# Unit 0's last product: planned fp32 columns, or rounded products in the mixed stretch

## The chip, the cores and the metric

One core of a Trainium2 chip runs the whole kernel. The metric is the time of one execution in device microseconds. The engines are TensorE (PE in the profile; PEld is its weight load), VectorE (DVE), ScalarE (ACT), GpSimd (POOL) and SyncE (SP), which issues most DMAs.

## What is computed

Three stages follow each other. Causal attention by blocks of 64 (4 batches, 8 heads, 576 positions, 64 wide) gives 2304 tokens of 512 values. A dense stage makes of each token

```python
h = np.maximum(np.maximum(x @ w1, x @ w2), x @ w3)   # 512 -> 768, three matrices
x2 = h @ w_out                                       # 768 -> 512
```

and a routed stage sends each row of x2 to two of eight experts (512 to 1024 to 512), chosen from the logits `x2 @ w_gate` and `x2 @ w_noise`. The weights of the dense stage arrive as 8-byte floats, and the kernel makes 4-byte ones of them itself.

## The kernel before

The 2304 tokens are nine units of 256. A dense unit has two parts. Its hidden part takes three pairs of 128 hidden columns (fp = 0, 1, 2); for each it makes the products with w1, w2 and w3 in one PSUM bank each and takes the maximum of the three. Its columns part multiplies the maxima with w_out for two tiles of 128 tokens (tt = 0, 1). The 2 x 8 gate columns are w_out times the gate matrices, and are appended to w_out, so that a unit gives its routing logits beside x2.

Nearly all products are "rounded": an operand is split into a high part (rounded to fp32r by ScalarE, `hh` for the maxima) and a low part (the difference, by GpSimd or VectorE, `hl`), and one product becomes three (high x high, high x low, low x high), accumulated in one bank. A unit's columns are then, for each tt and each half of the 528 columns, 6 x 3 products of 264 columns (`columns`, lines 791 to 793), followed by a ScalarE copy to an `x2` tile (line 796) and a store.

Unit 0 is made in another way. It is computed before the weights are split, with plain fp32 products, of which the trace shows two records each: `first_hidden` (line 589), `first_max` (ScalarE copy, then two VectorE maxima, into the three `hh` buffers), then for each tt `first_columns` with w_out and again with the 16 gate columns (line 606), a ScalarE copy and a store.

All this stands in the planned stretch, `start()`, at the beginning. There the order on each engine is written by a small planner (`Plan.run`). Each operation has an engine, a cost in microseconds, the operations it waits for, and a time by which its result is late (0.1, for loads 2.0). An operation's level is the longest sum of cost and lateness from it to the end; whenever an engine is free in the planner's own clock, it takes the ready operation with the highest level. Attention jobs 4 to 7 get a tail of 15 on their last operation, `EX`. The planned operations are:

- the loads of 24 weight pieces by SyncE (`LD`), and their conversion: `integers` on VectorE, `low_bits` on ScalarE, `join` on GpSimd (`AD`). Pieces 0 to 17 are w1 to w3, by fp; 18 to 23 are the six 128-row blocks of w_out;
- the early attention jobs 0 to 7 (`LQ` and `LV` load, then scores, exponentials, scaling, transposes, values, `EX`). Jobs 0 to 3 give unit 0's input, 4 to 7 unit 2's;
- unit 0, as above;
- the splits of the weights (`part`: ScalarE, line 580, then GpSimd, line 578), with w_out last, as it waits for the products of w2 and w3 and the splits of w2 and w3;
- the gate columns (`gate_turn`, `gate_copy`, `gate_product`, `gate_out`).

Until the first `first_hidden`, holes of TensorE are filled with warm-up products (line 137).

Behind the planned stretch comes the mixed one. Attention jobs 8 to 31 are written one after the other, and between their steps `filler` takes steps from a generator, `chain`, which goes through the other dense units (2, 4, 1, 6, 3, 5, 7). The toolchain's scheduler then lays out the instructions of each engine. It keeps the order of the planned operations among themselves, but may place others between them where their data and buffers are there. Attention outputs of units 2, 4, 6 and 8 go to a ring of six buffers (`xA`), of which unit 2 has four before the mixed stretch.

Of the kernel before, what the change touches and what calls it, by code (L numbers as in the profile page):

```python
# [7 lines left out]
F32 = mybir.dt.float32  # L8
F32R = mybir.dt.float32r
# [13 lines left out]
UT = 256  # L23
# [31 lines left out]
class Plan:  # L55
# [5 lines left out]
    def add(self, engine, cost, emit, deps=(), prio=0.0, take=None, give=None, late=0.1):  # L61
        self.ops.append((engine, cost, emit, tuple(deps), prio, take, give, late))
        return len(self.ops) - 1
# [49 lines left out]
def plain(ap):  # L113
    return ap.bitcast(F32)
# [3 lines left out]
def tile_attention_moe_moe(ctx, tc, qT, kT, v, w1, w2, w3, w_out, gates, noise, e1, e2, out):  # L118
# [113 lines left out]
    def bank(kind="m"):  # L232
        n, c = TAGS[kind]
        return (psS if n == "s" else psT).tile([128, 512], F32, name=n, bufs=c)
# [186 lines left out]
    def new_x(u, g):  # L421
        if u == 8:
            return keep.tile([128, 2, D], F32R, name="xs")
        if u == 0:
            if g % 2 == 0:
                XT["0"] = moe.tile([128, 2, UT], F32, name="hl", bufs=3)
            XT[u, g] = XT["0"][:, g % 2]
            return XT[u, g]

        if u == 5:  # L430
            XT[u, g] = att.tile([128, 2, UT], F32R, name=("qe", "kve", "pe", "pte")[g])
            return XT[u, g]
        r = 0 if u in RINGS[0] else 1
        n = 4 * RINGS[r].index(u) + g - XBUF[r]
        while n >= 0 and RINGS[r][n // 4] not in done:
            next(fill)
        XT[u, g] = moe.tile([128, 2, UT], F32R, name=("xA", "xB")[r], bufs=XBUF[r])
        return XT[u, g]
# [149 lines left out]
        for kt in range(4):  # L588
            nc.tensor.matmul(H0[-1][:, j], WP[MATS[m][0]][:, kt, f:f + 128], XT[0, kt], start=kt == 0, stop=kt == 3)

    M0 = []

    def first_max(fp, m):
        ps = H0[3 * fp + m]
        if m == 0:
            M0.append(moe.tile([128, 2, UT], F32, name="hh", bufs=3))
            nc.scalar.activation(M0[fp], ps, AF.Copy)
        else:
            nc.vector.tensor_max(M0[fp], ps, M0[fp])

    C0 = {}

    def first_columns(tt, w, n):
        ps = C0["p"] = bank()
        for ft in range(6):
            nc.tensor.matmul(ps[:, :n], M0[ft // 2][:, ft % 2, tt * 128:tt * 128 + 128], w[ft], start=ft == 0,
                             stop=ft == 5)

    def first_out(tt):
        x2 = C0[tt] = keep.tile([128, DM], F32, name="x2", bufs=2)  # L610
        nc.scalar.activation(x2, C0["p"], AF.Copy)

    def first_gates(tt):
        if "g" not in C0:
            C0["g"] = logits()
        nc.vector.tensor_copy(C0["g"][:, tt], C0["p"][:, :2 * E])

    def first_load(j, eng, half):
        i = at(j)
# [8 lines left out]
    def start():  # L628
# [71 lines left out]
            work(n, 10.0 + n)  # L700

        hid, mats = [], [[], [], []]
        prev = None
        for fp in range(3):
            for m in range(3):
                d = [AD[6 * fp + 2 * m], AD[6 * fp + 2 * m + 1]] + [EX[j] for j in range(4)]
                a = add("PE", 1.73, lambda fp=fp, m=m: first_hidden(fp, m, 0), d + hid[-1:], 100.0, take="t")
                b = add("PE", 1.73, lambda fp=fp, m=m: first_hidden(fp, m, 1), [a], 99.0)
                hid.append(b)
                mats[m].append(b)  # L710
                prev = add("DVE" if m else "ACT", 0.6, lambda fp=fp, m=m: first_max(fp, m), [b] + ([prev] if m else []),
                           24.0, give="t")
        sp = {}

        def part(key, n, i, j, src, deps, prio, cost):
# [26 lines left out]
            done_g = go[-1]  # L742
        so = [part(None, "o", f, slice(0, DM), WPO[f], mats[1] + mats[2] + sp[1] + sp[2], 55.0, 1.26) for f in range(6)]
        part(None, "o", slice(0, 6), slice(DM, NG), WPG, so + go, 55.0, 0.4)
        last = prev
        for tt in range(2):
            a = add("PE", 5.2, lambda tt=tt: first_columns(tt, WPO, DM), [last, prev] + [AD[n] for n in range(18, 24)], 100.0, take="t")
            last = add("ACT", 0.75, lambda tt=tt: first_out(tt), [a], 24.0, give="t")
            add("SP", 0.7, lambda tt=tt: store(0, tt, C0[tt]), [last], 24.0)
            a = add("PE", 1.3, lambda tt=tt: first_columns(tt, [WPG[:, ft] for ft in range(6)], 2 * E), [last] + go, 100.0, take="t")  # L750
            last = add("DVE", 0.2, lambda tt=tt: first_gates(tt), [a], 24.0, give="t")
        for j in range(4, 8):
            pl.tail[EX[j]] = 15.0
        return pl, idle, hid[0]
# [49 lines left out]
    def logits():  # L804
        return keep.tile([128, 2, 2 * E], F32, name="gl", bufs=2)

    def moe1(u):
        parts = []
        yield from hidden(u, parts)
        done.add(u)  # L810
        yield 0.01
        gl = logits()
        for tt in range(2):
            x2 = keep.tile([128, DM], F32, name="x2", bufs=2)
            for c in (0, 264):
                columns(parts, tt, c, 264, x2, gl)
                yield 2.0
            store(u, tt, x2)
        late.append(route(u, gl))
        yield 0.1  # L820


# [140 lines left out]
    ready = set()  # L963

    def chain():
        for u in CH:
            while u not in ready:
                yield None
            yield from moe1(u)
# [59 lines left out]
    psA.append(ph1.enter_context(tc.tile_pool(name="psA", bufs=1, space=bass.MemoryType.PSUM)))  # L1029
    init_route()  # L1030
    init_ids()
    late.append(route(0, C0["g"]))
    done.add(0)
    ready.add(2)
    load_scores(EJ[0])
    load_rest(EJ[0])
# [371 lines left out]
```

## Time and profile before

| | |
|---|---|
| median of three timed runs | 1019.64 us (1015.58 to 1020.12) |
| the profiled execution | 1013.09 us |
| its span, first to last instruction | 1011.3 us |
| TensorE: matmuls, weight loads busy | 982.2 us, 894.9 us |
| VectorE, ScalarE, GpSimd busy | 479.6 us, 424.6 us, 457.2 us |
| mean granted TensorE clock | 0.995 |

Matmuls are pipelined, so a record is longer than the step to the next one; the time that a run of matmuls takes is read from start times. The profile's times are counted from the start of the span.

### The profile page before, as it was taken

What the parts mean: (1) busy time and instruction counts of PE and PEld (TensorE: products, weight loads), DVE (VectorE), ACT (ScalarE), POOL (GpSimd) and SP (SyncE); (2) the same over time, 40 slices, a digit from 0 to 9 for tenths busy, and PEclk for the clock granted to TensorE, in tenths of its full rate; (3) what the DMA queues carried; (4) which work ended last, traced back from release to release, by engine and by line L of the source; (5) the groups of instructions that cost most, each with busy time, mean ns of one, the idle gap of its engine ahead of it and who ended that gap; (6) DMA issues with size and microseconds to landing.
All of it is one profiled execution on the core that took longest, in us unless ns stands there. A gap on an engine that the chain in (4) does not pass through costs nothing. (4 is left out here: it accounts for less than half of the span.)

```text
span 1011.3 us, 17379 instructions
## 1 busy us (share of the span) xinstructions
PE 982.2 (97%) x6557; PEld 894.9 (88%) x6557; DVE 479.6 (47%) x1320; ACT 424.6 (42%) x1005; POOL 457.2 (45%) x381
## 2 busy tenths in 40 slices
PE   8989999999999999999998899999999999999997
PEld 4776898999999999999997789899898989888895
DVE  6873658766688787863245331132222222222221
ACT  5687447555556666642122333332331314232210
POOL 2777132241324334331224487774755647574302
PEclk9999999999999999999999999999999999999999
DMA  8931315221012221212001466554434435342101
GB/s 257 297 124 52 109 36 198 69 56 43 25 56 69 64 60 35 70 37 97 23 22 53 130 218 192 176 173 151 159 105 152 144 120 190 98 171 85 53 19 57
DMA packets 76264, 107.32 MB, mean 106 GB/s; under 512 B 23672, under 2 KB 48248, under 8 KB 76176
## 3 DMA queue, kind: packets, MB, share of 16 engines
q1 hardware_dynamic: 63408, 75.97, 24.4%
q0 software_dynamic: 10592, 29.41, 8.9%
q8 instruction: 53, 0.87, 0.4%
q10 hardware_dynamic: 2176, 0.79, 0.3%
q14 instruction: 35, 0.29, 0.1%
HBM read 86.66 MB, written 20.53 MB: 106 GB/s over the span
## 5 line engine op out<-in xcount | busy, mean ns | idle before, releaser
L179 POOL TENSOR_TENSOR w<-rw,w 128x1536 fp32r<-128x1536 f32 (+1 forms) x45 | 141.1, 3145 | 73.6 <-ACT w L178 59.2
L178 ACT ACTIVATE w<-rw 128x1536 fp32r<-128x1536 f32 (+1 forms) x45 | 60.5, 1344 | 101.9 <-DMA rw<-in_e 53.2
L1138 PE MATMUL b<-xh,w 128*128 128x384 f32 (+7 forms) x272 | 87.5, 323 | 0.7 <-ACT xh L1128 0.7
L1139 PE MATMUL b<-xl,w 128*128 128x384 f32 (+7 forms) x272 | 87.5, 322 | 0.0
L1140 PE MATMUL b<-xh,w 128*128 128x384 f32 (+7 forms) x272 | 87.4, 322 | 0.0
L767 PE MATMUL t<-xA,w 128*128 128x256 f32 x288 | 82.5, 286 | 0.0
L768 PE MATMUL t<-xA,w 128*128 128x256 f32 x288 | 81.8, 284 | 0.0
L769 PE MATMUL t<-xA,w 128*128 128x256 f32 x288 | 81.5, 283 | 0.0
L1187 POOL DMA_INDIRECT out_rows<-y,isc x40 | 40.6, 1014 | 78.9 <-DVE y L1186 72.1
L1143 DVE SCALAR_TENSOR_TENSOR ht<-b,ht 128x384 fp32r<-128x384 f32 (+6 forms) x56 | 29.1, 519 | 96.6 <-ACT ht L1142 96.6
L782 POOL TENSOR_TENSOR hl<-hm,hh 128x512 fp32r<-128x512 f32 x21 | 27.5, 1311 | 98.4 <-ACT hh L781 98.2
L1140 PE MATMUL t<-xh,w 128*128 128x256 f32 x240 | 67.4, 281 | 0.0
L1139 PE MATMUL t<-xl,w 128*128 128x256 f32 x240 | 67.3, 281 | 0.0
L1182 PE MATMUL b<-w,ht 128*128 128x512 f32 (+1 forms) x168 | 67.0, 399 | 0.0
L1138 PE MATMUL t<-xh,w 128*128 128x256 f32 x240 | 66.9, 280 | 0.0
L1184 PE MATMUL b<-w,ht 128*128 128x512 f32 (+1 forms) x168 | 66.4, 395 | 0.0
L1183 PE MATMUL b<-w,ht 128*128 128x512 f32 (+1 forms) x168 | 66.3, 394 | 0.0
L271 POOL TENSOR_TENSOR Kl<-rk,Kh 128x576 fp32r<-128x576 f32 x16 | 23.2, 1451 | 93.6 <-ACT Kh L270 93.6
L1186 DVE SCALAR_TENSOR_TENSOR y<-b,idt,prev 128x512 f32<-128x512 f32 (+1 forms) x24 | 18.0, 750 | 97.8 <-PE b L1184 71.0
L767 PE MATMUL t<-xB,w 128*128 128x256 f32 x216 | 61.3, 284 | 0.0
L768 PE MATMUL t<-xB,w 128*128 128x256 f32 x216 | 61.3, 284 | 0.0
L769 PE MATMUL t<-xB,w 128*128 128x256 f32 x216 | 61.2, 283 | 0.0
(421 smaller groups left out, 3077.6 us busy)
## 6 DMA issues: line engine op xcount, KB each, us to landing
rw<-in_e SPq DMA_DIRECT2D x32, 768.0 KB, 4.7
w<-in_w SPq DMA_DIRECT2D x18, 512.0 KB, 9.2
rw<-in_e SPq DMA_DIRECT2D x16, 512.0 KB, 3.7
rv<-in_v SPq DMA_DIRECT2D x16, 320.0 KB, 2.9
rk<-in_kT SPq DMA_DIRECT2D x16, 288.0 KB, 3.4
x2d<-x SPq DMA_DIRECT2D x18, 256.0 KB, 2.2
out_rows<-x SPq DMA_DIRECT2D x9, 512.0 KB, 3.3
w<-in_w_out SPq DMA_DIRECT2D x6, 512.0 KB
```

What stands on the lines that cost most here:

```text
L178: nc.scalar.activation(t[:, 0, :c], r[:, :c], AF.Copy)
L179: nc.gpsimd.tensor_sub(t[:, 1, :c], r[:, :c], plain(t[:, 0, :c]))
L767: nc.tensor.matmul(ps[:, j], wh, x[:, 0], start=kt == 0, stop=False)
L768: nc.tensor.matmul(ps[:, j], wh, x[:, 1], start=False, stop=False)
L769: nc.tensor.matmul(ps[:, j], wl, x[:, 0], start=False, stop=kt == 3)
L1138: nc.tensor.matmul(p, wt1(e, 0, kt, f), th[:, kt, c0:c1], start=kt == 0, stop=False)
L1139: nc.tensor.matmul(p, wt1(e, 0, kt, f), tl[:, kt, c0:c1], start=False, stop=False)
L1140: nc.tensor.matmul(p, wt1(e, 1, kt, f), th[:, kt, c0:c1], start=False, stop=kt == 3)
L1182: nc.tensor.matmul(ps, a, wt2(e, 0, f), start=f == 0, stop=False)
L1183: nc.tensor.matmul(ps, a, wt2(e, 1, f), start=False, stop=False)
L1184: nc.tensor.matmul(ps, l, wt2(e, 0, f), start=False, stop=f == 7)
L1187: st = nc.gpsimd.indirect_dma_start(out=out, out_offset=bass.IndirectOffsetOnAxis(ap=isc[:n, e, c:c + 1], axis=0), in_=y, in_offset=None, ...
```

## The change

Unit 0's columns leave the plan. `first_columns`, `first_out` and `first_gates` go. The maxima go to two `hm` buffers instead of three `hh`, and two new operations split each pair: `first_high` (ScalarE) and `first_low` (VectorE). The low parts of the first two pairs use the two `xA` buffers that unit 2 leaves free, the third an `hl` buffer. Unit 0's columns are then made as those of the other units, by a new generator `rows_out`, which is the second half of what was `moe1`, and which `chain` takes first of all. An attention output that would go into one of the two `xA` buffers waits until that is done.

```diff
         r = 0 if u in RINGS[0] else 1
         n = 4 * RINGS[r].index(u) + g - XBUF[r]
+        while n >= -2 and r == 0 and 0 not in done:
+            next(fill)
...
-    M0 = []
+    M0, P0 = [], []
...
-            M0.append(moe.tile([128, 2, UT], F32, name="hh", bufs=3))
+            M0.append(moe.tile([128, 2, UT], F32, name="hm", bufs=2))
...
-    def first_columns(tt, w, n):
-    def first_out(tt):
-    def first_gates(tt):
...
+    def first_high(fp):
+        a = moe.tile([128, 512], F32R, name="hh", bufs=3).rearrange("p (a b) -> p a b", a=2)
+        l = (moe.tile([128, 512], F32R, name="hl", bufs=3).rearrange("p (a b) -> p a b", a=2) if fp == 2 else
+             moe.tile([128, 2, UT], F32R, name="xA", bufs=XBUF[0]))
+        P0.append((a, l))
+        nc.scalar.activation(a, M0[fp], AF.Copy)
+
+    def first_low(fp):
+        nc.vector.tensor_sub(P0[fp][1], M0[fp], plain(P0[fp][0]))
...
+            a = add("ACT", 0.6, lambda fp=fp: first_high(fp), [prev] + (hid[-1:] if fp == 2 else []), 26.0)
+            low.append(add("DVE", 0.75, lambda fp=fp: first_low(fp), [a], 26.0))
...
-        last = prev
-        for tt in range(2):
-            a = add("PE", 5.2, lambda tt=tt: first_columns(tt, WPO, DM), [last, prev] + [AD[n] for n in range(18, 24)], 100.0, take="t")
-            last = add("ACT", 0.75, lambda tt=tt: first_out(tt), [a], 24.0, give="t")
-            add("SP", 0.7, lambda tt=tt: store(0, tt, C0[tt]), [last], 24.0)
-            a = add("PE", 1.3, lambda tt=tt: first_columns(tt, [WPG[:, ft] for ft in range(6)], 2 * E), [last] + go, 100.0, take="t")
-            last = add("DVE", 0.2, lambda tt=tt: first_gates(tt), [a], 24.0, give="t")
...
     def chain():
+        yield from rows_out(0, P0)
         for u in CH:
...
-    late.append(route(0, C0["g"]))
-    done.add(0)
```

`first_max` of the last pair's first matrix also waits for the first `first_low`, as it takes that pair's `hm` buffer.

## Rows read from the trace of the kernel before

**Rows 1.** The page's busy times, share of the span, instructions.
```profile
PE 982.2 (97%) x6557; PEld 894.9 (88%) x6557; DVE 479.6 (47%) x1320; ACT 424.6 (42%) x1005; POOL 457.2 (45%) x381
```
**Rows 2.** Table by stretches: length, busy time of each engine, clock, DMA.
```profile
29.30:88.30 59.00, 53.62 (x296) 45.09 (x295) 40.23 (x90) 44.96 (x120) 41.54 (x38) 1.00 0.54 170
88.30:106.30 18.00, 18.00 (x89) 12.11 (x88) 5.89 (x14) 7.70 (x19) 12.05 (x12) 1.00 0.22 67
106.30:450.00 343.70, 339.87 (x2669) 327.71 (x2669) 257.30 (x761) 203.60 (x548) 105.36 (x112) 1.00 0.23 67
```
**Rows 3.** Timeline of TensorE, 87 to 107 us: start, length, instructions.
```profile
87.44 0.39 PE L292 MATMUL s<-Kh,Qh 128*128 128x320 f32 x1
...
88.28 4.45 PE L606 MATMUL t<-xB,hh 128*128 128x512 f32 x10
...
93.43 0.27 PE L553 MATMUL t<-ident,xB 128*128 128x128 f32 x1
...
97.13 1.49 PE L606 MATMUL t<-xs,hh 128*128 128x16 f32 x12
98.47 4.54 PE L606 MATMUL t<-xB,hh 128*128 128x512 f32 x10
...
103.70 1.41 PE L606 MATMUL t<-xs,hh 128*128 128x16 f32 x12
104.96 0.85 PE L403 MATMUL t<-ident,pe 128*128 128x128 f32 x6
...
106.34 0.28 PE L767 MATMUL t<-xA,w 128*128 128x256 f32 x1
```
**Rows 4.** Table by stretches, either side of 60 us.
```profile
29.30:60.00 30.70, 28.79 (x134) 24.35 (x133) 25.90 (x42) 17.58 (x34) 24.14 (x23) 1.00 0.92 298
60.00:92.00 32.00, 28.53 (x172) 22.43 (x171) 14.34 (x49) 29.93 (x91) 21.11 (x20) 1.00 0.14 36
```
**Rows 5.** Timeline of GpSimd, 63 to 101 us; brackets: idle before, ended by.
```profile
63.49 1.04 POOL L544 TENSOR_TENSOR hl<-w 128x512 int32<-128x512 int32 x1
...
70.55 1.27 POOL L578 TENSOR_TENSOR w<-w 128x512 fp32r<-128x512 f32 x1
82.17 4.96 POOL L578 TENSOR_TENSOR w<-w 128x512 fp32r<-128x512 f32 x4 [10.35 <-ACT w L580]
...
92.57 6.21 POOL L578 TENSOR_TENSOR w<-xB,w 128x512 fp32r<-128x512 f32 x5
...
99.94 0.41 POOL L578 TENSOR_TENSOR w<-xs,w 128x96 fp32r<-128x96 f32 x1
```
**Rows 6.** Timeline of TensorE, unit 2's columns; 16 products between these lines.
```profile
159.88 0.28 PE L791 MATMUL t<-w,hh 128*128 128x264 f32 x1
...
161.94 0.29 PE L793 MATMUL t<-w,hl 128*128 128x264 f32 x1
162.06 0.31 PE L294 MATMUL s<-Kl,Qh 128*128 128x320 f32 x1
```
**Rows 7.** Groups of instructions: count, busy us, mean ns, idle before.
```profile
L781 ACT ACTIVATE hh<-hm 128x512 fp32r<-128x512 f32 x17 | 10.7, 629 | 8.9 <-DVE hm L774 8.7
...
L381 DVE TENSOR_TENSOR Pl<-t,Ph 128x512 fp32r<-128x512 f32 x47 | 31.8, 684 | 5.6 <-ACT Ph L380 5.0 <-issue 0.4
...
L611 ACT ACTIVATE x<-t 128x512 f32<-128x512 f32 x2 | 1.2, 598 | 8.3 <-PE t L606 8.3
```
**Rows 8.** Timelines of SyncE's issues and of TensorE: job 4.
```profile
33.53 1.26 SPq L247 DMA_DIRECT2D Qh<-in_qT  x2
...
50.38 0.92 PE L332 MATMUL s<-Kh,Qh 128*128 128x256 f32 x4
```
**Rows 9.** Timeline of ScalarE: the output of attention job 8.
```profile
117.50 0.38 ACT L454 ACTIVATE xA<-t 128x256 fp32r<-128x256 f32 x1 [2.55 <-PE t L446]
```
**Rows 10.** Table by stretches, TensorE alone: length, busy time, granted clock, DMA.
```profile
534.00:536.00 2.00, 0.52 (x4) 1.00 0.04 2
536.00:538.00 2.00, 2.00 (x14) 0.71 0.21 53
538.00:540.00 2.00, 2.00 (x11) 0.50 0.77 155
```

More of the change, by code (lines that the diff above doesn't have):

```diff
@@ L599, in first_max @@
             nc.vector.tensor_max(M0[fp], ps, M0[fp])
-    C0 = {}
-    def first_columns(tt, w, n):
[L604 to L607, printed above, removed]
-    def first_out(tt):
-        x2 = C0[tt] = keep.tile([128, DM], F32, name="x2", bufs=2)
-        nc.scalar.activation(x2, C0["p"], AF.Copy)
-    def first_gates(tt):
-        if "g" not in C0:
-            C0["g"] = logits()
-        nc.vector.tensor_copy(C0["g"][:, tt], C0["p"][:, :2 * E])
+    def first_high(fp):
[6 more added lines that the diff above has]
+        nc.vector.tensor_sub(P0[fp][1], M0[fp], plain(P0[fp][0]))
     def first_load(j, eng, half):
@@ L702, in start @@
         hid, mats = [], [[], [], []]
-        prev = None
+        prev, low = None, []
         for fp in range(3):
@@ L710, in start @@
                 mats[m].append(b)
-                prev = add("DVE" if m else "ACT", 0.6, lambda fp=fp, m=m: first_max(fp, m), [b] + ([prev] if m else []),
+                prev = add("DVE" if m else "ACT", 0.6, lambda fp=fp, m=m: first_max(fp, m), [b] + ([prev] if m else []) + (low[:1] if fp == 2 and m == 0 else []),
                            24.0, give="t")
+            a = add("ACT", 0.6, lambda fp=fp: first_high(fp), [prev] + (hid[-1:] if fp == 2 else []), 26.0)
+            low.append(add("DVE", 0.75, lambda fp=fp: first_low(fp), [a], 26.0))
         sp = {}
@@ L811, in moe1, with rows_out @@
         yield 0.01
+        yield from rows_out(u, parts)
+    def rows_out(u, parts):
         gl = logits()
@@ L819, in moe1 @@
         late.append(route(u, gl))
+        done.add(u)
         yield 0.1
```

## The prediction

> **What bounds the kernel now.** I read the page's busy shares first: TensorE holds matmuls for 97% of the span [rows 1], so time is won where TensorE has fewer columns to stream or fewer holes. Then the table by stretches [rows 2]. From 106.3 to 450 us, where attention and the dense units are mixed, TensorE is idle for 343.70 - 339.87 = 3.8 us of 344: there, work taken away or added counts almost in full. From 29.3 us, where the first dense product starts, to 88.3 us it is idle for 59.0 - 53.62 = 5.4 us. From 88.3 to 106.3 it has no hole. The timeline of that last stretch [rows 3] shows what fills it: unit 0's columns, and little else.
>
> The second thing to see is which engine makes the planned stretch long. ScalarE is busy 29.93 of 32 us from 60 to 92 us, but only 17.58 of 30.7 us before that [rows 4]. GpSimd, which makes the low halves of the weights, stops at 71.8 us and starts again at 82.2; the bracket in its timeline puts those 10.35 us on a ScalarE split [rows 5]. Its last split of w_out, that of the gate columns, ends at 100.35 us. So the stretch is a ScalarE queue with a GpSimd tail, and the fp32 columns stand on TensorE while that tail runs.
>
> **Removed from TensorE.** By start times in [rows 3]: first token tile 88.28 to 93.43 = 5.15 us, its gate columns 97.13 to 98.47 = 1.34, second tile 98.47 to 103.70 = 5.23, its gates 103.70 to 104.96 = 1.26. Together 12.98 us, all in a stretch without a hole.
>
> **Added to TensorE.** Four groups of 18 products of 264 columns (2 token tiles, 2 column halves; the gate columns ride in the second half). The same group of unit 2 runs from 159.88 to 162.06 us with nothing between [rows 6]: 2.18 us, 0.121 us a product. Four groups are 8.72 us. As they stand at the head of the mixed work, everything of later units moves back by that. Net: 8.72 - 12.98 = -4.26 us.
>
> Here a page of the Trainium skill can be held against the rows. "Perfetto Trace Analysis", section "Engine Utilization", says in a footnote that the array's output rate is halved for FP32_LOW_HIGH. By that an estimate for twelve fp32 products of 512 columns is 5.1 us, less than the three-product form costs, and the change would lose. The trace disagrees, since the twelve took 10.38 us; the sum goes by the rows.
>
> **Added to ScalarE and VectorE.** Three first_high copies; the same form took 629 ns [rows 7], so 1.89 us. Two 512-wide copies of the result (598 ns each) go; four half-width copies come, in the mixed stretch, where ScalarE is busy 203.6 of 343.7 us [rows 2]. Three first_low subtractions on VectorE: the nearest row, the same size out of PSUM, is 684 ns [rows 7]; 2.05 us. VectorE is busy 14.34 of 32 us from 60 us on [rows 4], so that hides; uncovered it would be a chain of 0.68 us for the last pair. One first_high falls before 60 us, where ScalarE has 13 us of holes. The other two (1.26 us) can fall where ScalarE is full; without cover they push GpSimd's tail back by that much. Bounds 0 and 1.3; I take 0.5.
>
> **The plan is ordered anew.** The planner ranks by the longest chain of its own costs (plus 0.1 a step) to the end. With the column chain gone, 15.7 of planned cost (and 0.7 of the last maximum before it) no longer stands behind the last first_hidden; what is left is 2.7 of w_out's splits. I add up: that first_hidden falls from 20.1 to 6.4, the join of piece 12 from 28.5 to 14.9, the load of piece 10 from 37.1 to 23.4. Attention jobs 4 to 7 keep theirs, since their tail of 15 is written in: 23.0 for the scores, 26.9 for the query loads. So these jobs, which stood behind the weight pieces, now go ahead of them. In the trace job 4's query load is issued at 33.53 us and its first score runs at 50.38 [rows 8], after the loads of most weight pieces; and it is these jobs that fill ScalarE while GpSimd waits. Earlier jobs would use ScalarE's 13 us of holes before 60 us and shorten the wait of 10.35 us.
>
> What is it worth? TensorE's own work is unchanged, so only its 5.4 us of holes before 88.3 us can be won: at most -5.4 us. (Something of warm-up time before 29.3 us could be used too; I leave it out.) From the other side: the query, key and value loads go ahead of weight pieces in a stretch where DMA is busy 92% [rows 4], and the pieces come later. A late piece can open a hole as long as what it gained; +2 us. Near the middle, -2 us.
>
> **New wait: the columns need the split w_out.** Before, they read the fp32 w_out, whose last block is joined by 64.5 us. Now they read both halves, the last of which GpSimd ends at 100.35 us [rows 5]. With 12.98 us gone TensorE would come to them at about 106.34 - 12.98 = 93.4 us. GpSimd makes one block of 128 rows in 1.28 us, and the four groups eat a block with 12 products, 1.45 us, so they could run behind it; but the order is fixed before the run, and a matmul that waits holds all behind it. Bounds: nothing, when GpSimd's hole closes (100.35 - 10.35 = 90.0 us) or when unit 2's products, whose weights GpSimd splits before it comes to w_out at 92.57 us, are put in front; 100.35 - 93.4 = 7 us when neither happens. The order is the scheduler's, and it already puts scores of a later job ahead of the planned columns (87.44 us in [rows 3]), which is nearer to the first bound. I take 0.3.
>
> Behind a late first unit wait: attention job 8's output, which now needs a buffer that a low half had (that copy ran at 117.50 us [rows 9], so it has some 10 us), and in the same way unit 2's first high half. The two stores of unit 0 and its routing scatters on GpSimd move into the mixed stretch; they go to memory that is read only near the end. The x2 buffers are shared with the zero fills of the output, four evacuations long: nothing, as TensorE has four banks ahead.
>
> **Sum.** -4.26 + 0.5 - 2 + 0.3 = -5.5 us on the profiled 1013.09 us (span 1011.3 and 1.8 around it): 1007.6 us, a ratio of 0.9946. Only the ratio carries over, as the three timed runs lie above the profiled one; on their median it is 1014.1 us. About 0.5% (5.1 us) is what a measurement of this kernel can tell from no change, so the forecast lies on that edge.
>
> **Rivals.**
> 1. *The new order pays in full.* All 5.4 us of holes close and ScalarE's early holes also take some of the jobs' work into the warm-up. For: ScalarE's imbalance of 57% against 94%. Against: DMA at 92% before 60 us. -4.26 - 5.4 = -9.7 us: 1009.9.
> 2. *The wait for the split w_out takes the place of the fp32 columns.* For: its end at 100.35 us, and that the columns are first among the mixed work. Against: there is other work to put before it. A wait of 3 to 7 us in place of my 0.3: -2.8 to +1.2 us, and up to +2.8 with the clock's 1.6 us (rival 3); about 1019.
> 3. *Slower: the weight pieces become so late that the split w_out ends far after the place where unit 2 now starts.* Its splits are planned behind the last first_hidden, which lost its rank. TensorE then stands until GpSimd is done and has 1.45 us of last products left. Even with now is an end of GpSimd at 104.9 us; it is slower by 0.5% from 110 us on, 9.7 us later than today. A pause costs twice: after TensorE did 0.52 us of work from 534 to 536 us, its granted clock was 0.71 and then 0.50, the lower level of 1.2 GHz, over the next 4 us [rows 10], about 1.6 us of work lost. "TensorE: Matmul & The Clock Gate", section "Why this matters for your kernels", of the Trainium skill warns of such pauses; the trace agrees with the 0.50. Time: 1025 or more.
> 4. *The fp32 products hold TensorE for only half of what they show*, the rest being pipeline that the neighbours can use: 10.38 / 2 + 2.60 removed, 8.72 added, no gain of order, +0.9 us: 1020.6. The start times in [rows 3], which follow each other without a hole, speak against it. (It is also what the halved rate in "Perfetto Trace Analysis" of the Trainium skill would give.)
>
> **How the numbers follow.** Forecast (1011.5 to 1017) 0.42, of it 0.25 beyond the 0.5% (below 1014.5). Rival 1: 0.23, all faster. Rival 2: 0.25, within 0.5%, but for 0.02 faster. Rival 3: 0.08, slower. Rival 4: 0.02, same. So faster 0.50, same 0.42, slower 0.08. The time is that of the forecast, 1014.1. The range takes in rival 1 with some of the warm-up (1006) and rival 2's worse end (1019.6 + 2.8 = 1022); what is left out is rival 3 and the tails, under 0.15.
>
> **What would show it.** Line 606's products gone, and 72 more of lines 791 to 793, at 0.121 us; the first of them between 90 and 100 us. Unit 2's first product at 106.34 - 5.5 = about 101 us or, if it goes ahead of the columns, TensorE without holes around it. Job 4's first score well before 50 us. GpSimd's wait of 10.35 us shorter, its last split before 97 us. From there to the end each stretch as long as before. The prediction fails if TensorE shows a pause of over 2 us before a product of line 791 or 792 of unit 0, if the weight joins end much later than 64.5 us, or if the mixed stretch loses time that it did not lose before.

## The result, and the profile after

The changed kernel is slower: 1027.62 us (median of 4 runs, 1026.56 to 1033.69) against 1018.97 us, a ratio of 1.0105 with a 95% interval of 1.0079 to 1.0131. The forecast was 1014.1 us, the range ended at 1022, and "slower" had a chance of 0.08. (The two medians alone give 1.0085.) The profiled execution took 1028.36 us, with a span of 1026.6 us where before had 1011.3. The trace of the kernel before is of a quick execution (1013.09 us at a mean granted clock of 0.995; the four timed beside the change took 1015.58 to 1020.12 us), so of the 15.3 us between the two traces only some 10.7 (the ratio) are the change's.

The work itself changed as forecast. The page's busy line, to set beside [rows 1]:

```profile
PE 987.0 (96%) x6581; PEld 902.4 (88%) x6581; DVE 483.0 (47%) x1323; ACT 425.6 (41%) x1010; POOL 459.0 (45%) x381
```

TensorE has 24 instructions more (48 fp32 records fewer, 72 products more). Nothing in these totals explains the loss. The table by stretches does. First the 130 us from 20 us on, in the kernel before (length, then busy time of each engine, granted clock, DMA share, GB/s):

```profile
20.00:150.00 130.00, 123.96 (x776) 104.19 (x776) 83.85 (x223) 80.73 (x214) 70.42 (x66) 1.00 0.42 129
```

The same stretch after, and the two stretches of [rows 4]:

```profile
20.00:150.00 130.00, 113.36 (x686) 97.78 (x687) 81.66 (x203) 79.59 (x213) 65.45 (x60) 0.92 0.40 128
...
29.30:60.00 30.70, 24.92 (x108) 21.00 (x107) 22.61 (x50) 16.02 (x49) 12.20 (x13) 0.90 0.90 305
60.00:92.00 32.00, 26.11 (x146) 21.76 (x146) 18.89 (x42) 27.49 (x72) 21.36 (x19) 0.89 0.15 41
```

TensorE is idle 10.6 us more in these 130 us, and its granted clock is 0.92 where it was 1.00. Compare GpSimd with [rows 4]: from 29.3 to 60 us it is busy 12.20 us in place of 24.14. And ScalarE, which was to fill its early holes, is busy less there than before, 16.02 us in place of 17.58.

SyncE's issues show the new order: one weight piece (line 527) at 26.23 us, then twelve lines of query, key and value loads of attention jobs 4 to 7, the next piece at 36.73 us.

```profile
26.23 0.47 SPq L527 DMA_DIRECT2D w<-in_w  x1
26.79 1.27 SPq L247 DMA_DIRECT2D Qh<-in_qT  x2
...
36.21 0.46 SPq L252 DMA_DIRECT2D kve<-in_v  x1
36.73 0.97 SPq L527 DMA_DIRECT2D w<-in_w  x2
```

VectorE, which converts the pieces, then waits for one (the bracket: idle before, ended by what):

```profile
42.61 0.69 DVE L532 TENSOR_SCALAR sh<-w 128x512 int32<-128x512 int32 x1 [4.75 <-DMA w<-in_w]
```

GpSimd's timeline, to set beside [rows 5] (line 546 joins pieces, line 580 makes low halves):

```profile
44.16 1.04 POOL L546 TENSOR_TENSOR w<-w 128x512 int32<-128x512 int32 x1 [8.45 <-DVE w L533]
...
66.66 1.04 POOL L546 TENSOR_TENSOR w<-w 128x512 int32<-128x512 int32 x1 [5.45 <-DVE w L533]
...
80.37 1.04 POOL L546 TENSOR_TENSOR hl<-w 128x512 int32<-128x512 int32 x1
...
105.43 6.49 POOL L580 TENSOR_TENSOR w<-xB,w 128x512 fp32r<-128x512 f32 x5
...
113.12 0.54 POOL L580 TENSOR_TENSOR w<-xs,w 128x96 fp32r<-128x96 f32 x1
```

The last join starts at 80.37 us (63.49 before), and the last split of w_out ends at 113.66 us (100.35 before). Last, TensorE, to set beside [rows 8] and [rows 3]: job 4's first score, its new pauses with the unit 0 products (line 591) behind them, unit 0's columns (line 781), and unit 2's first product (line 757).

```profile
34.41 0.92 PE L332 MATMUL s<-Kh,Qh 128*128 128x256 f32 x4
...
40.14 1.89 PE L591 MATMUL t<-hl,w 128*128 128x256 f32 x8
46.01 1.07 PE L332 MATMUL s<-kve,qe 128*128 128x256 f32 x4 [3.99 <-ACT Ph L344]
46.88 3.58 PE L591 MATMUL t<-hl,w 128*128 128x256 f32 x8
...
56.59 0.72 PE L332 MATMUL s<-V 128*128 128x64 f32 x4 [1.79 <-ACT Ph L344]
57.11 3.58 PE L591 MATMUL t<-hl,w 128*128 128x256 f32 x8
...
65.19 2.69 PE L332 MATMUL s<-kve,qe 128*128 128x256 f32 x8 [3.40 <-DVE w L533]
...
103.08 0.37 PE L781 MATMUL t<-w,hh 128*128 128x264 f32 x1
106.20 0.81 PE L781 MATMUL t<-w,hh 128*128 128x264 f32 x2 [2.75 <-ACT w L582]
...
123.20 0.28 PE L757 MATMUL t<-xA,w 128*128 128x256 f32 x1
```

Job 4's first score came 16 us earlier, as forecast. But the scores of jobs 4 to 7 now stand in TensorE's fixed order ahead of unit 0's products, and wait there: by the brackets, two of the three pauses end with an exponential on ScalarE, the third with a piece's conversion on VectorE. Eight records behind such a pause take 3.58 us in place of 1.89, as the granted clock is 0.50 from 47 to 50 us, the lower level of 1.2 GHz. Unit 2 starts at 123.20 us, 16.9 us later than in [rows 3]. The last dense hidden product starts at 539.5 us against 527.5 (+12.0), and the span is 15.3 us longer.

### The profile page after: what moved, and what is told of

It is laid out like the page before. It is cut to its first block, busy times and chain, and to the rows that moved or that the text cites. A ratio compares the mean times of both kernels' runs of the same rounds, so it can differ in the third digit from the quotient of the medians.

```text
span 1026.6 us, 17409 instructions
## 1 busy us (share of the span) xinstructions
PE 987.0 (96%) x6581; PEld 902.4 (88%) x6581; DVE 483.0 (47%) x1323; ACT 425.6 (41%) x1010; POOL 459.0 (45%) x381
## 5 line engine op out<-in xcount | busy, mean ns | idle before, releaser
L781 PE MATMUL t<-w,hh 128*128 128x264 f32 x216 | 62.6, 293 | 3.5 <-ACT w L582 2.8
L782 PE MATMUL t<-w,hh 128*128 128x264 f32 x216 | 61.5, 287 | 0.0
L757 PE MATMUL t<-xB,w 128*128 128x256 f32 x216 | 61.4, 284 | 0.0
L758 PE MATMUL t<-xB,w 128*128 128x256 f32 x216 | 60.8, 281 | 0.0
```

The lines of the kernel that those rows point to most:

```text
L757: nc.tensor.matmul(ps[:, j], wh, x[:, 0], start=kt == 0, stop=False)
L758: nc.tensor.matmul(ps[:, j], wh, x[:, 1], start=False, stop=False)
L781: nc.tensor.matmul(ps[:, :n], a, wh, start=ft == 0, stop=False)
L782: nc.tensor.matmul(ps[:, :n], a, wl, start=False, stop=False)
```

## The experiments

Two theories stood at the start. **Order**: the planner's new order of the planned stretch costs the time. **Columns**: unit 0's columns, first in the mixed work, wait for the split w_out. Ratios are to the kernel before on the same chip (medians 1016.77 to 1017.86 us).

**Run 1, the change with the planner's ranks of before.** Tails put back by hand what the column chain had given.

```diff
+            prev_max = prev
...
+        pl.tail[prev_max] = 15.7
+        for x in go:
+            pl.tail[x] = 9.55
+        for n in range(18, 24):
+            pl.tail[AD[n]] = 15.7
```

> The change, with the planner's ranks of the kernel before put back by hand (tails of 15.7 on the last maximum and on the joins of w_out, 9.55 on the gate columns); the operations are those of the change. Theory 1, the lost rank put attention jobs 4 to 7 ahead of the weight pieces and that is the loss: the last join ends near 65 us instead of 81.4, unit 2's first product starts at 98 to 103 us instead of 123.2, the time is 0.993 to 0.998 of the kernel before. Theory 2, the loss is the columns' wait for the split w_out at the head of the mixed stretch: the pause before line 781 stays or grows to 3 to 7 us, and the time stays above 1.006.

Measured: 1019.07 us, ratio 1.0009 (0.9991 to 1.0026). The last join starts at 64.07 us, where before it was at 63.49, and with it all of the loss goes: 0.96 points. The gain did not come, and unit 2 starts at 108.79 us, later than the 98 to 103 expected. Unit 0's columns start at 96.42 us and wait twice (timelines of GpSimd and of TensorE):

```profile
64.07 1.03 POOL L546 TENSOR_TENSOR hl<-w 128x512 int32<-128x512 int32 x1
...
97.31 0.39 PE L788 MATMUL t<-w,hh 128*128 128x264 f32 x1 [0.15 <-POOL w L580]
...
98.54 0.39 PE L788 MATMUL t<-w,hh 128*128 128x264 f32 x1 [0.60 <-POOL w L580]
```

Ahead of them stands a pause of 1.14 us, at 85 us, and then half clock up to 94 us.

**Run 2, the order alone.** The kernel before, its planned fp32 columns kept, but their chain left out of the ranks.

```diff
+        n0 = len(pl.ops)
         for tt in range(2):
             a = add("PE", 5.2, lambda tt=tt: first_columns(tt, WPO, DM), ...
...
+        pl.cut = set(range(n0, len(pl.ops)))
...
+            if i in self.cut:
+                continue
             for d in self.ops[i][3]:
                 level[d] = max(level[d], level[i])
```

> The kernel before, with its fp32 columns in the plan, but its planner counts nothing for the column chain when it ranks, as in the change. Theory 1: the order of the change comes back without the change, last join at 78 to 83 us, time 1.006 to 1.014 of the kernel before (the holes and the halved clock of the stretch from 40 to 80 us, without the 4.3 us of shorter products). Theory 2: no more than 0.003 away from the kernel before.

Measured: 1023.70 us, ratio 1.0058 (1.0037 to 1.0078). That is at the lower edge of what was expected. With no change to any computation the order costs 0.6 points: its last join starts at 76.0 us and its last split at 107.1 us, and TensorE shows the same pauses (2.97, 2.57 and 3.76 us before the same scores).

```profile
76.01 1.03 POOL L546 TENSOR_TENSOR hl<-w 128x512 int32<-128x512 int32 x1
```

It costs less than in the changed kernel. Here the fp32 columns need no split, and no pause stands ahead of them, where the change has one of 2.75 us; that this is the whole difference is not shown.

**Run 3, the loads put behind the pieces.** The loads of jobs 4 to 7 wait for piece 15; their ranks on the engines stay high. The program also writes the jobs behind the conversions, which the lines below don't show.

```diff
-            LQ[j] = add("SP", 1.9, lambda: load_scores(j), [ES[old, 1]], p, late=2.0)
-            LV[j] = add("SP", 0.65, lambda: load_rest(j), [EV[old]], p, late=2.0)
+            LQ[j] = add("SP", 1.9, lambda: load_scores(j), [ES[old, 1], LD[15]], p, late=2.0)
+            LV[j] = add("SP", 0.65, lambda: load_rest(j), [EV[old], LD[15]], p, late=2.0)
```

> The change, but the loads of attention jobs 4 to 7 may be issued only after the load of weight piece 15; all ranks as in the change. If within theory 1 the loss came through the queue of SyncE (26.8 to 36.7 us taken by these loads while VectorE waits 4.7 us for a piece): the wait for a piece is gone, joins end before 70 us, time 0.994 to 1.001 of the kernel before. If it came through the ranks on VectorE, ScalarE and TensorE: the jobs still crowd out the pieces once loaded, joins after 75 us, time above 1.005. Theory 2: as the change, 1.008 to 1.013.

Measured: 1036.80 us (four executions), ratio 1.0164 (1.0119 to 1.0210), the slowest of all. Putting the loads back alone does not take the loss away: the last join starts at 84.20 us. With later data and the same high rank a score stands further in the way, for 5.94 us. But not all that this run lost is of that kind (timelines of TensorE and of VectorE):

```profile
52.82 1.86 PE L332 MATMUL s<-V 128*128 128x256 f32 x4 [5.94 <-ACT Ph L344]
...
98.23 11.47 DVE L611 TENSOR_TENSOR xA<-hm,hh 128x512 fp32r<-128x512 f32 x1 [0.79 <-ACT hh L608]
...
109.94 1.01 PE L565 MATMUL t<-p,p 128*128 128x16 f32 x4 [7.57 <-DVE xs L569]
```

One subtraction of first_low (line 611) took 11.47 us beside an unbroken row of GpSimd's splits, and a gate product waited 7.57 us for the VectorE copy behind it. This is a loss of its own, which neither theory had.

**Run 4, the columns later.** The change, with two of unit 2's hidden steps ahead of unit 0's columns.

```diff
-        yield from rows_out(0, P0)
         for u in CH:
             while u not in ready:
                 yield None
-            yield from moe1(u)
+            g = moe1(u)
+            if u == CH[0]:
+                for _ in range(2):
+                    yield next(g)
+                yield from rows_out(0, P0)
+            yield from g
```

> The change, with unit 0's columns placed behind the first two of unit 2's nine hidden steps (5.7 us of products that need no w_out); plan as in the change. Theory 1: only the pause of 2.75 us before the columns and part of the low clock behind it can go, 1.005 to 1.010 of the kernel before. Theory 2: most of the loss goes, 1.002 or less.

Measured: 1027.25 us, ratio 1.0064 (1.0027 to 1.0102; the medians alone give 1.0093). Its interval overlaps that of the change (1.0079 to 1.0131), so in this order no gain from the columns' place is shown. Of the ten executions four took 1016.51 to 1020.45 us and six 1027.00 to 1031.51. The traced one is among the six (1030.67 us), and it has the same long subtraction as run 3 (timelines of VectorE, TensorE and ScalarE):

```profile
85.90 11.24 DVE L611 TENSOR_TENSOR xA<-hm,hh 128x512 fp32r<-128x512 f32 x1
...
97.30 0.65 PE L555 MATMUL t<-ident,xB 128*128 128x128 f32 x4 [2.87 <-DVE xs L569]
...
97.24 0.60 ACT L599 ACTIVATE hm<-t 128x512 f32<-128x512 f32 x1 [7.38 <-DVE xs L569]
```

In the trace of the change the subtraction that starts at the same 85.90 us took 1.82 us. Whether the four are the executions without the long subtraction is not known, as only one execution was traced. The order theory stands, as the ratio stays above 1.002; how much the columns' place is worth in this order stays open.

**Run 5, ranks of before and columns later** (the edits of runs 1 and 4).

> The change with the planner ranks of the kernel before put back (as in the first run), and unit 0's columns taken behind the first two of unit 2's hidden steps. If the first run lost its gain at the columns' waits for the split w_out (0.15 and 0.60 us there) and at the half clock ahead of them, TensorE has unit 2's products to do meanwhile: 3 to 5 us faster than the first run, ratio to before about 0.997, and no wait on a GpSimd split. If the loss sits in the planned stretch itself (the pause at 85 us and the half clock behind it come before any column product), the time stays within 0.2% of the first run, ratio 1.000 to 1.002.

Measured: 1013.54 us, ratio 0.9962 (0.9944 to 0.9980), faster than both kernels. No column product waits, unit 2's first product is at 93.83 us, and the last group of all dense columns starts its last three products at 535.8 us, where the kernel before has them at 540.3 (timelines of TensorE, run 5 and the kernel before):

```profile
535.77 0.28 PE L787 MATMUL t<-w,hh 128*128 128x264 f32 x1
...
540.28 0.29 PE L791 MATMUL t<-w,hh 128*128 128x264 f32 x1
```

That is about the 4.3 us of the products themselves. Against run 1 the place of the columns is worth 0.47 points, and the two intervals do not meet.

**Run 6, one number.** The change, with the jobs' tail lowered by the 13.7 that the pieces lost.

```diff
         for j in range(4, 8):
-            pl.tail[EX[j]] = 15.0
+            pl.tail[EX[j]] = 1.3
```

> The change, with one number altered: the tail of attention jobs 4 to 7 is 1.3 in place of 15. That lowers these jobs by the 13.7 of planned cost that the weight pieces and unit 0's first products lost, so that jobs and pieces stand to each other as before. If the loss comes from the jobs' passing the pieces, joins end near 65 us, the last split of w_out by 104 us, and the time is that of the first run, ratio 0.997 to 1.004. If it comes from something else in the planner (the splits and gate products, which now rank above the jobs), joins end near 65 us all the same, but the ratio stays above 1.006.

Measured: 1017.84 us, ratio 0.9992 (0.9973 to 1.0012). The last join starts at 63.7 us and the last split ends at 98.69 us. One number takes the loss away, so it was the jobs' passing the weight pieces (timeline of GpSimd):

```profile
63.71 1.04 POOL L546 TENSOR_TENSOR hl<-w 128x512 int32<-128x512 int32 x1
```

**Run 7, the pauses filled.** The change, with warm-up products in two of TensorE's pauses.

```diff
+                n = {(7, 0): 17, (6, 1): 7}.get((j, h), 0)
-                s = ES[j, h] = add("PE", (0.76, 0.34)[h], lambda h=h: e_scores(j, h, sb),
+                s = ES[j, h] = add("PE", (0.76, 0.34)[h], lambda h=h, n=n: (warm(spare_bank, n), e_scores(j, h, sb)),
```

> The change as it is, with warm-up products of 0.22 us in two of TensorE's new pauses: 17 ahead of job 7's first score (pause of 3.99 us), 7 ahead of job 6's second (1.79 us). They compute nothing that is used. If the half clock of 1.2 GHz that follows the pauses is a cost of its own, the two groups of eight first_hidden records behind them take 1.9 us in place of 3.6 each and the time falls by 2 to 4 us, ratio to before about 1.007. If the order on ScalarE and GpSimd sets the end (joins at 81 us, last split at 113.7 us), the clock at 46 to 60 us is 1.00, TensorE waits that much longer later, and the time stays that of the change, 1.010.

Measured: 1027.50 us, ratio 1.0085 (1.0051 to 1.0118), not to be told from the change. From 40 to 60 us the clock came back (table by ten microseconds; columns as above):

```profile
40.00:50.00 10.00, 9.35 (x45) 6.22 (x45) 7.42 (x17) 5.76 (x17) 3.69 (x4) 1.00 1.02 376
50.00:60.00 10.00, 8.40 (x47) 6.29 (x45) 9.46 (x28) 7.93 (x31) 4.80 (x6) 1.00 1.02 372
...
90.00:100.00 10.00, 5.94 (x31) 4.46 (x29) 5.96 (x4) 5.20 (x10) 8.11 (x8) 1.00 0.00 2
```

The time did not. The last join still starts at 77.9 us and the last split at 115.9 us, and TensorE stands 4.1 us between 90 and 100 us instead. This run does not settle what the half clock costs, though: the granted clock was 0.83 from 60 to 80 and from 100 to 120 us, and one subtraction of first_low took 10.46 us, as in runs 3 and 4, with 2.08 us of TensorE's new idle time behind it. In the change's own trace it took 1.82 us.

**Run 8, run 1 with the pause filled.** Five warm-up products of 0.22 us ahead of the second gate product.

```diff
-            done_g = add("PE", 1.7, lambda g=g: gate_product(g), ...
+            done_g = add("PE", 1.7, lambda g=g: (warm(spare_bank, 5 if g == 1 else 0), gate_product(g)), ...
```

> The change with the ranks of before (first run), and five warm-up products of 0.22 us ahead of the second gate product, where that run showed a pause of 1.14 us and then a granted clock of 0.50 from 87 to 94 us. If the half clock is what ate the gain there (some 3.2 us of work lost), the clock stays at 1.00 and the kernel beats both: ratio to before 0.995 to 0.998, columns' first product near 93 us. But then the columns reach the split w_out earlier, and if GpSimd's last split (102.9 us) holds them, the wait grows by as much: ratio 1.000.

Measured: 1021.97 us, ratio 1.0037 (1.0017 to 1.0056): no faster than run 1, and rather slower (the two intervals overlap), which neither expectation had. The clock stayed at 1.00 to 90 us, the columns' first product came at 93.5 us in place of 96.4, and then waited 3.0 us for GpSimd, whose last split starts at 102.1 us as in run 1 (102.5):

```profile
95.69 0.39 PE L788 MATMUL t<-w,hh 128*128 128x264 f32 x1 [1.79 <-POOL w L580]
96.92 0.39 PE L788 MATMUL t<-w,hh 128*128 128x264 f32 x1 [0.60 <-POOL w L580]
98.15 0.59 PE L788 MATMUL t<-w,hh 128*128 128x264 f32 x1 [0.60 <-POOL w L580]
```

So the split w_out holds the columns in run 1 as well; the half clock hid most of that wait. Further pauses of 0.94 and 1.07 us follow at 119 and 121 us, which run 1 doesn't have in that form; why they come is open.

**Run 9, the engines alone.** Jobs 4 to 7 ranked 13.7 lower on TensorE, VectorE and ScalarE; SyncE's order in the plan is that of the change.

```diff
             loads(j)
+            n0 = len(pl.ops)
             job(j)
+            for x in range(n0, len(pl.ops)):
+                pl.plus[x] = -13.7
...
-                i = max(ready, key=lambda i: (level[i], -i))
+                i = max(ready, key=lambda i: (level[i] + self.plus.get(i, 0), -i))
```

> The change, with the operations of attention jobs 4 to 7 on TensorE, VectorE and ScalarE taken 13.7 lower in the planner, and their loads left where the change puts them: SyncE's order in the plan is that of the change. With the third run (loads put behind, engines left) and the sixth (both) it makes two by two. If the engines' order makes the loss (jobs' exponentials and scalings on ScalarE ahead of the pieces' low bits, and scores that stand in TensorE's queue ahead of unit 0's products), joins end below 72 us and the ratio to before is 0.998 to 1.004. If the weight pieces lose their time in SyncE's queue and the DMA, behind the jobs' query, key and value loads, joins still end at 78 us or later and the ratio is 1.007 to 1.011.

Measured: 1019.48 us, ratio 1.0039 (1.0009 to 1.0069). The last join starts at 64.9 us although GpSimd waits 7.49 us for its first late piece. With the change, run 3 and run 6 this makes two by two:

| | jobs high on the engines | jobs low on the engines |
|---|---|---|
| jobs' loads ahead of the pieces | 1.0105 (the change) | 1.0039 (run 9) |
| jobs' loads behind the pieces | 1.0164 (run 3) | 0.9992 (run 6) |

With the loads ahead, the engines' order makes some 0.7 of the 1.1 points. With the jobs low on the engines, the loads' place makes the other 0.5; the intervals of run 9 and run 6 overlap a little, so that this share is less sure. The field of run 3 says less: its trace has the long subtraction, which is neither order nor load, and its interval overlaps that of the change.

**Run 10, run 6 with the columns later** (run 4's edit).

> The change with both repairs in their simplest form: the jobs' tail 1.3 in place of 15 (ratio to before 0.9992 in the sixth run) and unit 0's columns behind the first two of unit 2's hidden steps, which was worth 0.41 and 0.47 points of the ratio in the two orders tried. If the two costs are independent, the ratio is 0.994 to 0.997 and no product of the columns waits for a GpSimd split. If the sixth run had already lost nothing at the columns (its last split ends at 98.3 us, its first column product at 97.4 us), it stays at 0.998 to 1.001.

Measured: 1016.48 us, ratio 0.9990 (0.9976 to 1.0004): nothing gained over run 6, the second of the two expectations. In run 6's order no column waits for a split, so there is nothing to win by moving them; its loss sits elsewhere. Part of it stands at a gate product, as these now rank above the jobs: in both runs one has 1.86 us of idle time before it (at 91.53 us in run 6), and the clock from 90 to 100 us is 0.66. The rest was not traced to its place.

**Run 11, run 5 with run 8's five products.**

> The fifth run (ranks of before, columns behind two of unit 2's hidden steps; ratio to before 0.9962) with the eighth run's five warm-up products ahead of the second gate product. The fifth run still showed the pause of 1.14 us there and a granted clock of 0.88 and 0.95 in the ten microseconds before and after 90 us, 1.7 us of work lost. Here nothing waits for a GpSimd split behind the pause, so if the half clock is a cost of its own wherever no later wait takes it back, the clock stays at 1.00 and unit 2's first product, at 93.8 us in the fifth run, comes 1 to 2 us earlier: ratio 0.9945 to 0.996. If the next hole takes it back here too, 0.996 to 0.998.

Measured: 1013.86 us, ratio 0.9967 (0.9951 to 0.9983), the same as run 5. The clock is 1.00 from 20 to 150 us, but unit 2 starts at 93.6 us, only 0.2 us before run 5. Later a score waits 2.00 us for a key load of a later attention job, a wait that run 5 does not have:

```profile
123.38 1.44 PE L332 MATMUL s<-kve,qe 128*128 128x256 f32 x8 [2.00 <-DMA kve<-in_kT]
```

## Why the prediction was wrong

**Removed and added: right.** In the sum this was -4.26 us. Run 5, in which neither order nor wait disturbs it, ends the dense columns 4.5 us earlier and has a ratio of 0.9962 (0.9944 to 0.9980), 3.9 us. A column product takes 0.12 us at full clock, as taken from [rows 6]. Rival 4, the fp32 products at half of what they show, would have made that +0.9 us; it is out.

**ScalarE and VectorE: right in sum, one size off.** The copies of first_high took 618 to 622 ns against 629 in [rows 7]. The subtractions of first_low took far more than the 684 ns of the nearest row (source view; minimum, median and maximum in ns):

```profile
L611 DVE TENSOR_TENSOR xA<-hm,hh x2: 1248/1534/1819, 85.9 to 95.1; 128x512 fp32r<-128x512 f32 x2
L611 DVE TENSOR_TENSOR hl<-hm,hh x1: 1474/1474/1474, 102.7 to 102.7; 128x512 fp32r<-128x512 f32 x1
```

That is 4.5 us in place of 2.05. In the change this cost no pause, and in run 5, where the last one took 1387 ns, no column waits. But "that hides" does not hold always: in the traces of runs 3, 4 and 7 one of them took 11.47, 11.24 and 10.46 us, and TensorE stood behind it for 7.57, 2.87 and 2.08 us. The nearest row, out of PSUM, could not show this; what it has to do with GpSimd stands in the last section.

**The plan ordered anew: the step that failed.** The ranks were worked out rightly, and so was who passes whom: the jobs' loads go at 26.79 us, the first score at 34.41 us, in place of 33.53 and 50.38 in [rows 8]. Wrong was the worth of it: -2 us, with +2 us as the worse end. Taking the order away is worth 9.8 us (1.0105 to 1.0009 of 1018 us) in the changed kernel, and 5.9 us in the old one (run 2). The reasoning had looked at ScalarE's 13 us of early holes and at the DMA, and asked what earlier jobs would fill. It did not ask what they would hold up. On TensorE their scores stand in a fixed order ahead of unit 0's products, and each waits for an exponential. On ScalarE and VectorE they go ahead of the conversion of the pieces, from which the joins, unit 0's products, the splits of w1 to w3 and, last of all, those of w_out follow. ScalarE got emptier before 60 us, not fuller (16.02 us busy in place of 17.58): it waited itself, once 5.14 us for a weight piece and once 3.01 us for a job's row maximum from VectorE. TensorE's 5.4 us of holes in [rows 2] were what could be won; what could be lost was GpSimd's whole chain, and this had no bound from the rows.

**The wait for the split w_out: the size was off.** The forecast took 0.3 us of the range 0 to 7, because the scheduler could put other work ahead. It did not: in the change the columns waited 2.75 us (the bracket names the ScalarE half of a w_out split), in run 1 0.75 us and in run 8 3.0 us (GpSimd's half). Moving them is worth 4.8 us in the order of before (0.47 points, run 5 against run 1), the cost that rival 2 described; the remedy is the one that was named for this step, unit 2's products put in front. In the change's order run 4 shows no such gain beyond its noise.

**Which rival came true.** Rival 3, and by its own mark: it was to be slower by 0.5% once GpSimd's last split ended at 110 us or later, and to take 1025 us or more. That split ended at 113.66 us and the median is 1027.62. It said that the weight pieces become late, and they did. The lateness itself the prediction had put on the loads that go ahead; the runs put the larger share on the engines' order (run 9). The rival's second price, the half clock behind a pause, is in the trace (3.58 us in place of 1.89), but filling pauses gave no time back in runs 7, 8 and 11. "TensorE: Matmul & The Clock Gate" of the Trainium skill, section "Why this matters for your kernels", advises against idle gaps between bursts of products. The traces agree that the clock can fall behind one, also behind gaps shorter than the page has in mind (1.14 us in run 1). None of the three runs shows that filling a pause shortens the kernel: in runs 8 and 11 another wait came instead, and run 7 had the long subtraction.

Of the three signs that the prediction had named for its failure two came: a pause over 2 us ahead of unit 0's columns (2.75 us), and joins that end at 81.4 us instead of 64.5. The third did not: the mixed stretch lost nothing, and takes 416.3 us from unit 2's first to the last dense hidden product, where it took 421.2.

**What stays open.** Which executions have the long subtraction, and whether those of the change that were not traced have it, is not known. Behind the dense units the traces differ by 3.3 us more (12.0 at the last hidden product, 15.3 at the end), and run 5 gave its whole 4.5 us back there in its profiled execution, though not in its median. That the trace of the kernel before lies below its median has a share in both. In the change and in run 5 the clock is at the lower level just as the routed stage starts (0.50 from 556 to 562 us in the change), where in the kernel before it had fallen, and come back, ahead of that [rows 10]. TensorE also waits longer there for the rows that the routed stage gathers: 1.73 and 1.48 us in the change, 1.81 and 1.20 us in run 5, 0.20 and 0.78 us before. Whether these come together in most executions was not tried.

## What to carry to other kernels

An operation that leaves a planned schedule takes its rank from everything that stood ahead of it. Before the change is costed, recompute the ranks and ask of each operation that moves up not only which hole it fills but which chain it now holds, down to that chain's last product. Where a planner has a constant written in by hand (here a tail of 15), it was set against the ranks of the day: restoring the difference, one number, took back a full per cent.

Where a product starts to need something that is made late, put work that doesn't need it in front; here two steps of the next unit turned no gain into 0.4%. And filling a pause won nothing where something late stood behind it (runs 8 and 11). An operation that is given to an engine because it is idle needs a second look at what runs beside it: VectorE had room for three subtractions, and beside GpSimd's splits one of them could take 11 us.

## What the runs showed of the hardware

**VectorE and GpSimd hold each other up.** The same subtraction of two operands in SBUF took VectorE 681 to 683 ns in run 1 for the first two pairs, and up to 1819 ns in the change. In run 3 it took 11.47 us, in run 4 11.24 and in run 7 10.46. In run 1 the first of them, at 53.3 us, was quick, and GpSimd's split that started beside it took 1.81 us (timeline of GpSimd):

```profile
53.33 1.81 POOL L580 TENSOR_TENSOR w<-w 128x512 fp32r<-128x512 f32 x1
...
59.59 1.27 POOL L580 TENSOR_TENSOR w<-w 128x512 fp32r<-128x512 f32 x1
```

The same split takes 1.27 us when no such subtraction stands beside it: 0.54 us more for the one, or, in the change, some 0.6 to 1.1 us more for the other. The rows show that at least one of the two pays when they overlap. The three long ones show that VectorE can pay far more. Each ended 0.55 or 0.56 us after the end of a row of GpSimd instructions without a gap between them, here of run 4 (timeline of GpSimd; the subtraction ran from 85.90 to 97.14 us):

```profile
84.67 3.77 POOL L580 TENSOR_TENSOR w<-w 128x512 fp32r<-128x512 f32 x3
88.36 0.89 POOL L286 TENSOR_TENSOR V<-rv,V 128x320 fp32r<-128x320 f32 x1
89.18 7.41 POOL L580 TENSOR_TENSOR w<-w 128x512 fp32r<-128x512 f32 x6
```

In the change the subtraction from 95.14 us ended in 1.25 us within such a row, so that it does not always come out this way; what decides it is open. "SBUF — State Buffer" of the Trainium skill, section "Terms", says that the two engines share a pair of ports which one holds for a whole instruction while the other is blocked; the rows agree as far as they show one standing for the other, but in run 4 VectorE stood for a row of GpSimd's instructions and not for one.

**The same pause did not always bring the same clock.** In the kernel before, TensorE has 1.14 us of idle time between 84 and 86 us. Its clock stays at 1.00 (table by single microseconds):

```profile
84.00:85.00 1.00, 0.49 (x4) 0.17 (x2) 0.00 (x0) 1.00 (x5) 1.00 (x2) 1.00 0.00 0
85.00:86.00 1.00, 0.37 (x4) 0.37 (x4) 0.43 (x2) 1.00 (x4) 1.00 (x2) 1.00 0.28 74
...
88.00:89.00 1.00, 1.00 (x5) 0.64 (x5) 0.00 (x0) 1.00 (x3) 1.00 (x2) 1.00 0.00 0
```

In run 1 a pause of 1.14 us stands in the same place, between the same products (values of an attention job before it, the second gate product and then scores behind it), and the clock falls to 0.50, the level of 1.2 GHz, until 94 us:

```profile
85.00:86.00 1.00, 0.17 (x2) 0.00 (x0) 0.17 (x1) 1.00 (x5) 1.00 (x2) 1.00 0.00 0
86.00:87.00 1.00, 0.69 (x6) 0.69 (x7) 0.58 (x2) 1.00 (x4) 1.00 (x2) 1.00 0.48 131
87.00:88.00 1.00, 1.00 (x8) 1.00 (x8) 0.85 (x3) 1.00 (x4) 1.00 (x2) 0.64 0.00 0
88.00:89.00 1.00, 1.00 (x6) 1.00 (x6) 0.01 (x1) 0.94 (x3) 1.00 (x1) 0.50 0.00 0
```

It falls while the gate product runs, before any product that the other kernel doesn't have. The pause starts 0.7 us later there, and the shorter pauses from 55 to 70 us are not quite the same; whether either decides it was not tried. So a pause's length alone does not price it. The executions of one kernel can differ in the clock as well: in run 9 the spans go from 1012.1 us at a mean granted clock of 0.992 to 1024.9 us at 0.983.
